# Small loads of one head's V: six rows and 192 keys instead of five rows and 128

## The chip, the cores and the metric

The kernel runs on one core of a Trainium2 chip. The metric is the device time of one execution in microseconds; the number given for a kernel is the median of its runs. A profile is taken of one further execution. "Granted clock" is the share of full speed that TensorE was allowed.

The core's engines are TensorE (PE, with its weight loads as PEld), VectorE (DVE), ScalarE (ACT), GpSimd (POOL) and SyncE (SP). Data come from the chip's memory (HBM) through 16 DMA engines. Here SyncE issues nearly all loads, on one queue.

## The reference

A decode step of two layer kinds, each done twice: attention over the last 1,024 positions of a key and value cache, and a gated feed-forward block. Four sequences, one token each, all in float32.

```python
def _A_ref(x, k_cache, v_cache, wq, wo):          # x 4 x 1 x 640, 32 heads of 128
    W = min(4096, max(256, Sk // 4))              # 1024
    q = (x @ wq).reshape(B, Sq, Hq, Dh)...
    k = k_cache[:, :, Sk - W:, :]
    v = v_cache[:, :, Sk - W:, :]
    scores = einsum("bhqd,bhkd->bhqk", q, k) * (Dh ** -0.5)
    p = softmax(scores, axis=-1)
    o = einsum("bhqk,bhkd->bhqd", p, v)
    return o... @ wo
def _B_ref(x, W_gate, W_up, W_down):              # 640 -> 1728 -> 640
    gate = x @ W_gate; up = x @ W_up
    return ((gate * (gate > 0)) * up) @ W_down
x = x + _A_ref(_layernorm(x), ...)
x = x + _B_ref(_layernorm(x), ...)
x = x + _A_ref(_layernorm(x), ...)
x = x + _B_ref(_layernorm(x), ...)
```

Both layers have the same weights and the same cache. Keys and values of the 1,024 positions are 128 KB x 32 heads x 4 sequences x 2, weights some 25 MB more.

## The kernel before

**Layout.** On the host everything is laid out as long rows of float32 on 128 partitions: `heads` (queries' weights, keys, values and output weights of most heads, in order of use), `kept` (those of the last two groups of heads, which stay on chip between the layers), `mlp`, and `limbs` (below). One head's V is 4,096 columns: eight blocks of 128 keys, each block 512 columns (four sequences of 128), with the key within the block on the partition.

**Store and plan.** `store` is one big tile of 50,304 columns (`STORE`) on all partitions, used as a ring. A list `plan`, written out ahead, has every load in order: layer, row, first and last column, place in the store. `stretch` (line 144) fills the main part: it cuts the `heads` row into loads of at most 16,064 columns (`MOST`, 64,256 B in a partition). `load` (line 226) issues from the front of the plan as long as the places are free; a place is freed by `part_done` after the product that read it (the chip's waits follow from that). So all loads stand on SyncE's queue in the order of the plan, and each waits for the space it goes to.

**Heads and values.** Heads are done in groups of up to four. `values` (line 463) multiplies the softmax weights of a group with V: for each head it copies the weights to a tile `pT`, then does eight products, one a block, into the bank `po`. The results of two rows of blocks add up on four groups of 32 rows of `po`.

**The split head.** Head 17 (`SPLIT`) isn't loaded like the others. Its last block of 128 keys (512 columns) isn't in `heads`: the host puts it into `limbs`, as seven runs of keys (`RUNS`), six of 20 and one of 8. The runs stand on partitions 0 to 19 and 32 to 51, in columns of 512 each. Thirteen small loads a layer (`LIMBS`) bring them to the last 2,048 columns of the store (`PART`): eight loads of five rows with 6 KB a row, and five with two rows or one, 2 KB a row. The rows of one load are four partitions apart, for instance 0, 4, 8, 12 and 16. `stretch` puts one of them ahead of the last big load but two of its stretch (up to the end of head 17), six ahead of the last but one, and six ahead of the last.

Because the keys of a run are on other partitions than their weights, `values` first moves the weights for head 17: a product of `to[:, 7]` with columns of the identity for each run (line 476), into a bank, and a copy to `pT` (line 485). Then come seven whole products and seven products over 20 or 8 partitions (line 490). After these, `free` gives the place back.

Of the kernel before, what the change touches and what calls it, by code (L numbers as in the profile page):

```python
# [13 lines left out]
B, D, H, DH, W, F = 4, 640, 32, 128, 1024, 1728  # L14
P = 128
# [11 lines left out]
KV = 4096  # L27
HEADS = [list(range(h, h + 4)) for h in range(0, 24, 4)] + [[24, 25, 26], [27, 28, 29], [30, 31]]
SIDE = 4
# [32 lines left out]
STORE = 50304  # L62
# [8 lines left out]
FIRST, MOST = 32128, 16064  # L71
LAP = 3 * MOST
SPLIT, PART = 17, 2048
LIMBS = [(half + i, 5, 0, 1536) for i in range(4) for half in (0, 32)] + [(i, 2, 1536, PART) for i in range(3)] + [(3, 1, 1536, PART), (7, 1, 1536, PART)]
RUNS = [(half, 20, 512 * s, 40 * s + 20 * (half > 0)) for s in range(3) for half in (0, 32)] + [(0, 8, 1536, 120)]


def size_of(what, i):
    if what == "v" and i == SPLIT:
        return KV - 512  # L80
    return len(HEADS[i]) * D if what == "q" else D if what == "o" else KV


def fewest(lo, end, n):

    if n == 1:
        return (0, [end]) if end - lo <= MOST else (n + len(CUTS), [])
    most = min(lo + MOST, end)
    ends = [(most, most not in CUTS)] + [(x, False) for x in CUTS if most - 512 < x < most]
    return min((fewest(hi, end, n - 1)[0] + cut, [hi, *fewest(hi, end, n - 1)[1]]) for hi, cut in ends)  # L90
# [23 lines left out]
def decode_kernel(ctx: ExitStack, tc: tile.TileContext, x, source, out):  # L114
    nc = tc.nc
# [10 lines left out]
    store = big.tile([P, STORE], F32, name="store")  # L126
# [7 lines left out]
    plan = []  # L134

    def put(layer, row, to, *cuts):

        for lo, hi in zip(cuts, cuts[1:]):
            assert 0 < hi - lo <= MOST and to % 64 == 0 and lo % 32 == hi % 32 == 0 and to + hi - lo <= STORE, (row, lo, hi, to)
            plan.append((layer, row, lo, hi, to))  # L140
            to += -(-(hi - lo) // 64) * 64
        return to

    def stretch(layer, lo, end, to):

        loads = []
        for hi in fewest(lo, end, -(-(end - lo) // MOST))[1]:
            if to + hi - lo > LAP:
                to = 0
            loads.append((lo, hi, to))  # L150
            to, lo = to + hi - lo, hi
        last = next(i for i, (lo, hi, _) in enumerate(loads) if lo < at_part("v", SPLIT) + KV - 512 <= hi)
        for i, (lo, hi, at) in enumerate(loads):
            if last - 3 < i <= last:
                half = (i - last + 1) * 6 + 1
                plan.extend((layer, "limbs", p, p + 1, STORE - PART) for p in range(max(half, 0), half + 6))
            put(layer, "heads", at, lo, hi)
        return to

    def at_part(what, i):  # L160
        return WHERE[what, i][1]

    def near(c, row="heads"):

        return max(x for x in ROWS[row][2] if x <= c)
# [9 lines left out]
    to = stretch(0, HELD, turn, FIRST)  # L175
# [7 lines left out]
    f, z, a, q, k = FRONT, STORE - D, AHEAD[0], AWAY[0], BACK[0]  # L183
# [4 lines left out]
    lo = 0  # L188
# [6 lines left out]
    lo = HELD  # L195
# [3 lines left out]
    to = AHEAD[1]  # L199
    for n in 832, 1280, 1024, 2048, 3392:  # L200
        to = put(1, "heads", to, lo, lo + n)
        lo += n
    assert to == HOME
    to = HOME + BACK[1] - BACK[0]
    for n in 4096, 6144, 9728:
        hi = near(lo + n)
        to = put(1, "heads", to, lo, hi)
        lo = hi
    hi = near(lo + 4608)
    to = put(1, "heads", to, lo, hi)  # L210
    lo, hi = hi, near(hi + STORE - to)
    put(1, "heads", to, lo, hi)
    last = near(heads_end - 25216)
    to = stretch(1, hi, last, 0)
    for lo, hi in (last, near(last + 12800)), (near(last + 12800), heads_end):
        to = put(1, "heads", to if to + hi - lo <= STORE else 0, lo, hi)
    cuts = [0, 7040, 12160, GU0 + 3 * GU, WD1 + WD, MLP - 4 * D, MLP - 2 * D, MLP - D, MLP - QUARTER, MLP]
    for lo, hi in zip(cuts, cuts[1:]):
        to = put(1, "mlp", to if to + hi - lo <= STORE else 0, lo, hi)
# [6 lines left out]
    def load():  # L226

        if not held:
            nc.sync.dma_start(out=first_q, in_=source["heads"][:, :HELD])
        while plan:  # L230
            layer, row, lo, hi, to = plan[-1]
            if any(live[to:STORE if row == "limbs" else to + hi - lo]):
                break
            plan.pop()
            if row == "limbs":
                live[to:STORE] = [lo == len(LIMBS) - 1] * PART
                p, n, a, b = LIMBS[lo]
                nc.sync.dma_start(out=store[p:p + 4 * n - 3:4, to + a:to + b], in_=source[row][p:p + 4 * n - 3:4, a:b])  # L238
                continue
            live[to:to + hi - lo] = [True] * (hi - lo)  # L240
            held.setdefault((layer, row), []).append((lo, hi - lo, to))
            nc.sync.dma_start(out=store[:, to:to + hi - lo], in_=source[row][:, lo:hi])
# [27 lines left out]
    def product(out, by, layer, row, lo, n, start, stop, rows=slice(0, P), **how):  # L270

        a = 0
        while a < n:
            t, p, m = place(layer, row, lo + a)
            z = min(n, a + m)
            nc.tensor.matmul(out[:, a:z], by, t[rows, p:p + z - a], start=start and not a, stop=stop and z == n, **how)  # L276
            a = z
# [18 lines left out]
    def part(layer, what, h, lo, n):  # L296
        row, first = WHERE[what, h]
        return layer, row, first + lo, n

    def part_done(layer, what, h, lo, n):  # L300
        row, first = WHERE[what, h]
        done(layer, row, first + lo, n)
# [18 lines left out]
    GAP = SIDE * B - B  # L321
# [6 lines left out]
    po = ps_o.tile([P, 512], F32, name="po")  # L328
# [5 lines left out]
    def bank(n):  # L334

        turn_of[0] ^= 1
        return banks[turn_of[0]][:, :n]
# [5 lines left out]
    ident, sel_q = sel_sb[:, :P], sel_sb[:, P:]  # L343
# [6 lines left out]
    for g in range(4):  # L350
        nc.tensor.matmul(y[32 * g:32 * g + B], ident[:B, :B], probs[:B, g * QUARTER:(g + 1) * QUARTER],
                         start=True, stop=True, tile_position=(0, 32 * g))
# [53 lines left out]
    qp, nm, sums, sc, r, oT = {}, {}, {}, {}, {}, {}  # L406
# [56 lines left out]
    def values(layer, g, last=False):  # L463


        n = len(HEADS[g])
        for i, h in enumerate(HEADS[g]):
            t = pT[i % 2]
            to = t[:, GAP:].rearrange("p (c x) -> p c x", c=8)[:, :, :B]
            nc.vector.tensor_copy(to, pp.rearrange("p j (c x) -> p (j c) x", c=4)[:, :, i:P:32])  # L470
            whole = 7 if h == SPLIT else 8
            if h == SPLIT:
                assert 0 < i < n - 1 and (layer, "limbs") not in [p[:2] for p in plan]
                limbs = bank(4 * B).rearrange("p (s x) -> p s x", s=4)
                for p, m, at, key in RUNS:
                    nc.tensor.matmul(limbs[p:p + m, at // 512], ident[:, key:key + m], to[:, 7],
                                     start=True, stop=True, tile_position=(0, p))
            for c in range(whole):
                a = c % 4
                at = GAP + SIDE * B * c - B * i  # L480
                product(po[32 * a:32 * a + SIDE * B], t[:, at:at + SIDE * B], *part(layer, "v", h, c * 512, 512),
                        start=i == 0 and c < 4, stop=i == n - 1 and c >= 4, tile_position=(0, 32 * a))
                part_done(layer, "v", h, c * 512, 512)
            if h == SPLIT:
                nc.vector.tensor_copy(to[:52, :4], limbs[:52])
                for p, m, first, _ in RUNS:
                    r = slice(p, p + m)
                    a = first // 512 % 2 + p // 16
                    at = GAP + SIDE * B * (first // 512) - B * i
                    nc.tensor.matmul(po[32 * a:32 * a + SIDE * B], t[r, at:at + SIDE * B],  # L490
                                     store[r, STORE - PART + first:STORE - PART + first + 512],
                                     start=False, stop=False, tile_position=(p, 32 * a))
                free(STORE - PART, STORE)
        if last:
            waits[0] = layer == 0
            fill(1, pp[:, 0])
            nc.vector.tensor_copy(gates[:, 2 * P:], po[:, 2 * P:])  # L497
            nc.scalar.copy(gates[:, :2 * P], po[:, :2 * P])
            if layer == 0:
                nc.gpsimd.tensor_copy(pT[0][:, GAP:], store[:, AHEAD[0] + INSIDE:AHEAD[0] + INSIDE + P])  # L500
                rest = AHEAD[1] - AHEAD[0] - INSIDE - P
                nc.vector.tensor_copy(pT[1][:, GAP:GAP + rest], store[:, AHEAD[1] - rest:AHEAD[1]])
                free(*AHEAD)
                nc.scalar.copy(po[:, P:], store[:, BACK[0] + 1024:BACK[0] + 1408])
                nc.scalar.copy(pp[:, :, 256:], away[:, :512].rearrange("p (j n) -> p j n", j=2))
                free(*BACK)
        else:
            nc.scalar.copy(gates, po)  # L508
# [167 lines left out]
    last = first_q[96:96 + B, QUARTER:2 * QUARTER]  # L676
# [58 lines left out]
```

## Time and profile before

| | before |
|---|---|
| median of 3 runs | 729.62 us (729.48 to 730.85) |
| profiled execution, its own time | 729.74 us |
| its span, first to last instruction | 727.9 us |
| granted clock, mean | 0.815 |
| TensorE busy | 450.0 us (62%) |
| VectorE, ScalarE busy | 70.5 us, 54.5 us |
| read from HBM | 310.32 MB, 426 GB/s over the span |
| SyncE's queue: packets, share of 16 DMA engines | 13,392, 99.2% |
| instruction packets (queue q8) | 30, 0.49 MB |
| issues of small loads | 26 (16 of 30 KB, 6 of 4 KB, 4 of 2 KB) |

The profiled execution's own time is 1.8 us over its span. Line numbers are those of the kernel's file; line 276 is in the helper that does most products, lines 238 and 242 are the two issues of loads, small and big. A DMA packet is one contiguous row of a load on one DMA engine. In rows by stretches of time, the first numbers are busy times of PE, PEld, DVE, ACT and POOL with counts, then the granted clock, the mean busy share of the 16 DMA engines and what they moved; a packet counts in the stretch in which it starts, so that a share can be over 1 in a short one.

### The profile page before, as it was taken

What the parts mean: (1) busy time and instruction counts of PE and PEld (TensorE: products, weight loads), DVE (VectorE), ACT (ScalarE), POOL (GpSimd) and SP (SyncE); (2) the same over time, 40 slices, a digit from 0 to 9 for tenths busy, and PEclk for the clock granted to TensorE, in tenths of its full rate; (3) what the DMA queues carried; (4) which work ended last, traced back from release to release, by engine and by line L of the source; (5) the groups of instructions that cost most, each with busy time, mean ns of one, the idle gap of its engine ahead of it and who ended that gap; (6) DMA issues with size and microseconds to landing.
All of it is one profiled execution on the core that took longest, in us unless ns stands there. A gap on an engine that the chain in (4) does not pass through costs nothing.

```text
span 727.9 us, 8368 instructions
## 1 busy us (share of the span) xinstructions
PE 450.0 (62%) x3824; PEld 146.9 (20%) x3824; DVE 70.5 (10%) x217; ACT 54.5 (7%) x102; POOL 2.4 (0%) x14
## 2 busy tenths in 40 slices
PE   3546565654645574619868896475756556558576
PEld 1111111111111121103334241021211012102123
DVE  2010001000010000001111211000000010001011
ACT  2000000000000000000412210000000000000100
POOL 0000000000000000000000000000000000000000
PEclk9567888887777787759999999677777878769989
DMA  9999999999999999999999999999999999999997
GB/s 409 444 394 447 440 444 434 412 435 444 443 428 416 421 457 418 444 422 426 418 414 412 426 431 452 429 441 433 434 423 440 438 436 417 441 444 423 425 420 312
DMA packets 13442, 310.91 MB, mean 427 GB/s; under 512 B 1576, under 2 KB 1916, under 8 KB 7136
## 3 DMA queue, kind: packets, MB, share of 16 engines
q1 hardware_dynamic: 13392, 310.37, 99.2%
q8 instruction: 30, 0.49, 0.2%
q14 instruction: 4, 0.03, 0.0%
q10 hardware_dynamic: 16, 0.01, 0.0%
HBM read 310.32 MB, written 0.05 MB: 426 GB/s over the span
## 4 chain that ended last, share of the span: by engine, by line
DMA 77%; PE 20%; DVE 1%; issue 1%; SPq 1%; ACT 0%; DVEq 0%; ACTq 0%
DMA store<-in_heads 62%; DMA store<-in_kept 9%; PE ps L276 8%; DMA store<-in_mlp 6%; PE po L276 6%; PE m L276 2%; PE y L276 1%; PE pp L276 1%; PE pp L461 1%; PE po L490 0%; PE m L432 0%; SPq L238 0%; PE po L358 0%; PE m L521 0%; PE m L512 0%
## 5 line engine op out<-in xcount | busy, mean ns | idle before, releaser
L276 PE MATMUL po<-store,pT 128*16 128x512 f32 x1026 | 157.9, 711 | 120.9 <-DMA store<-in_heads 115.2
L276 PE MATMUL ps<-store,qT 128*4 128x512 f32 (+2 forms) x998 | 152.7, 698 | 101.0 <-DMA store<-in_heads 80.7
L276 PEld LDWEIGHTS po<-store,pT 128*16 128x16 f32 x1026 | 33.4, 109 | 229.5 <-DMA store<-in_heads 126.7
L276 PEld LDWEIGHTS ps<-store,qT 128*4 128x4 f32 x998 | 30.8, 94 | 204.3 <-DMA store<-in_heads 91.8
L457 ACT ACTIVATE probs<-ps,nm 128x1024 f32<-128x1024 f32 x17 | 18.9, 1113 | 334.6 <-DVE nm L453 334.6
L453 DVE TENSOR_REDUCE nm<-ps 128x1 f32<-128x1024 f32 x17 | 20.8, 1225 | 233.9 <-PE ps L276 233.9
L276 PE MATMUL m<-store,xT 128*32 128x512 f32 (+3 forms) x146 | 27.9, 580 | 20.8 <-DMA store<-in_heads 20.8
L276 PE MATMUL y<-store,oT 128*4 128x160 f32 x512 | 23.2, 313 | 10.2 <-DMA store<-in_heads 8.9
L508 ACT COPY gates<-po 128x512 f32<-128x512 f32 x16 | 9.4, 586 | 256.5 <-PE po L276 256.5
L276 PE MATMUL pp<-store,xT 128*32 128x256 f32 (+2 forms) x320 | 20.3, 351 | 9.2 <-DMA store<-in_mlp 4.7
L470 DVE COPY pT<-pp 128x32 f32<-128x32 f32 x64 | 10.3, 184 | 143.5 <-PE po L276 126.4
L461 PE MATMUL pp<-sel_sb,probs 128*128 128x128 f32 x144 | 21.3, 297 | 0.0
L461 PEld LDWEIGHTS pp<-sel_sb,probs 128*128 128x128 f32 x144 | 18.7, 156 | 0.0
L514 DVE RECIPROCAL r<-m 128x16 f32<-128x16 f32 x18 | 4.6, 257 | 123.5 <-PE m L512 123.5
L276 PEld LDWEIGHTS y<-store,oT 128*4 128x4 f32 x512 | 12.7, 89 | 18.4 <-DMA store<-in_heads 9.2
L425 DVE TENSOR_SCALAR gates<-m,rstd 128x512 f32<-128x512 f32 (+2 forms) x18 | 12.4, 690 | 27.1 <-PE m L276 27.1
L276 PEld LDWEIGHTS pp<-store,xT 128*32 128x32 f32 x320 | 10.4, 109 | 17.7 <-DMA store<-in_mlp 8.5
L432 PE MATMUL m<-sel_sb,gates 128*128 128x128 f32 x64 | 12.7, 324 | 0.3 <-DVE gates L425 0.3
L276 PEld LDWEIGHTS m<-store,xT 128*32 128x32 f32 x146 | 6.0, 113 | 32.4 <-DMA store<-in_heads 23.3
L521 PE MATMUL m<-sel_sb,gates 128*128 128x128 f32 x72 | 11.9, 288 | 0.8 <-DVE gates L497 0.8
L432 PEld LDWEIGHTS m<-sel_sb,gates 128*128 128x128 f32 x64 | 7.9, 160 | 19.7 <-issue 18.9
L276 PE MATMUL y<-store,gates 128*4 128x160 f32 (+2 forms) x188 | 9.8, 296 | 1.7 <-DMA store<-in_mlp 1.1
(91 smaller groups left out, 135.7 us busy)
## 6 DMA issues: line engine op xcount, KB each, us to landing
store<-in_heads SPq DMA_DIRECT2D x15, 7936.0 KB
store<-in_heads SPq DMA_DIRECT2D x6, 8032.0 KB
store<-in_heads SPq DMA_DIRECT2D x2, 8000.0 KB
store<-in_heads SPq DMA_DIRECT2D x1, 7872.0 KB
store<-in_heads SPq DMA_DIRECT2D x1, 7424.0 KB
store<-in_heads SPq DMA_DIRECT2D x1, 7360.0 KB
store<-in_heads SPq DMA_DIRECT2D x1, 7168.0 KB
store<-in_heads SPq DMA_DIRECT2D x1, 6400.0 KB
```

Source lines behind the costliest of these rows:

```text
L276: nc.tensor.matmul(out[:, a:z], by, t[rows, p:p + z - a], start=start and not a, stop=stop and z == n, **how)
L425: nc.vector.tensor_scalar(gates[:, :len(HEADS[g]) * P], qp.pop(g), rstd, SCALE, op0=ALU.mult, op1=ALU.mult)
L432: nc.tensor.transpose(qt[:, i], gates[:, i * P:(i + 1) * P], ident)
L453: nc.vector.tensor_reduce(nm[g], to.rearrange("p j n -> p (j n)"), axis=AX.X, op=ALU.max, negate=True)
L457: nc.scalar.activation(probs, sc.pop(g).rearrange("p j n -> p (j n)"), AF.Exp, bias=nm.pop(g), accum_out=sums[g])
L461: nc.tensor.transpose(pp[:, c // 4, c % 4 * P:c % 4 * P + P], probs[:, c * P:(c + 1) * P], ident)
L470: nc.vector.tensor_copy(to, pp.rearrange("p j (c x) -> p (j c) x", c=4)[:, :, i:P:32])
L508: nc.scalar.copy(gates, po)
L514: nc.vector.reciprocal(r[g], so.rearrange("p (b i) -> p i b", b=B)[:, :SIDE])
L521: nc.tensor.transpose(ot[:, 127 * b:127 * b + P], gates[:, b * P:(b + 1) * P], ident)
```

## The change

Head 17's V keeps six whole blocks in `heads`. The seventh block and the eighth are split: 192 of their 256 keys, the whole eighth block and the first 64 keys of the seventh, go through the small loads, now eight runs of 24 keys on partitions 0 to 23 and 32 to 55. There are eight loads of six rows with 8 KB a row. The other 64 keys of the seventh block stay on partitions 64 to 127 and come in one load of 64 rows with 2 KB a row. That makes nine small loads a layer, three ahead of each of the same three big loads.

Since the `heads` row is 512 columns shorter, some big loads of the two stretches are cut elsewhere: in layer 0 the three after the small loads have rows of 62,976, 63,488 and 63,488 B where they had 64,256, 64,256 and 63,488; in layer 1 six loads from the first of these on have 63,488, 64,256, 64,256, 63,488, 63,488 and 51,200 B, before 64,256 four times, 64,000 and 51,200.

In `values`, head 17 takes nine products to move weights (a run can have keys of both blocks), six whole products, one over partitions 64 to 127 and eight over 24 partitions.

```diff
-LIMBS = [(half + i, 5, 0, 1536) for i in range(4) for half in (0, 32)] + [(i, 2, 1536, PART) for i in range(3)] + [(3, 1, 1536, PART), (7, 1, 1536, PART)]
-RUNS = [(half, 20, 512 * s, 40 * s + 20 * (half > 0)) for s in range(3) for half in (0, 32)] + [(0, 8, 1536, 120)]
+LIMBS = [(half + i, 6, 4, 0, PART) for i in range(4) for half in (0, 32)] + [(64, 64, 1, 0, 512)]
+RUNS = [(half, 512 * s) for s in range(4) for half in (0, 32)]
+MOVES = [(*RUNS[i], 24, 7, 24 * i) for i in range(5)] + [(*RUNS[6], 24, 6, 0), (*RUNS[7], 24, 6, 24), (*RUNS[5], 24, 6, 40), (*RUNS[5], 8, 7, 120)]
...
-        return KV - 512
+        return KV - 1024
...
-                half = (i - last + 1) * 6 + 1
-                plan.extend((layer, "limbs", p, p + 1, STORE - PART) for p in range(max(half, 0), half + 6))
+                plan.extend((layer, "limbs", p, p + 1, STORE - PART) for p in range(len(LIMBS)) if p // 3 == i - last + 2)
...
-                p, n, a, b = LIMBS[lo]
-                nc.sync.dma_start(out=store[p:p + 4 * n - 3:4, to + a:to + b], in_=source[row][p:p + 4 * n - 3:4, a:b])
+                p, n, by, a, b = LIMBS[lo]
+                rows = slice(p, p + by * (n - 1) + 1, by)
+                nc.sync.dma_start(out=store[rows, to + a:to + b], in_=source[row][rows, a:b])
...
-            whole = 7 if h == SPLIT else 8
+            whole = 6 if h == SPLIT else 8
...
-                for p, m, at, key in RUNS:
-                    nc.tensor.matmul(limbs[p:p + m, at // 512], ident[:, key:key + m], to[:, 7],
+                for p, at, m, c, key in MOVES:
+                    nc.tensor.matmul(limbs[p:p + m, at // 512], ident[:, key:key + m], to[:, c],
                                      start=True, stop=True, tile_position=(0, p))
...
-                nc.vector.tensor_copy(to[:52, :4], limbs[:52])
-                for p, m, first, _ in RUNS:
-                    r = slice(p, p + m)
+                at = GAP + SIDE * B * 6 - B * i
+                nc.tensor.matmul(po[64:64 + SIDE * B], t[64:, at:at + SIDE * B], store[64:, STORE - PART:STORE - PART + 512],
+                                 start=False, stop=False, tile_position=(64, 64))
+                nc.vector.tensor_copy(to[:56, :4], limbs[:56])
+                for p, first in RUNS:
+                    r = slice(p, p + 24)
```

The host's part lays the same keys out in `limbs`, now 128 rows.

More of the change, by code (lines that the diff above doesn't have):

```diff
@@ L151, in stretch @@
             to, lo = to + hi - lo, hi
-        last = next(i for i, (lo, hi, _) in enumerate(loads) if lo < at_part("v", SPLIT) + KV - 512 <= hi)
+        last = next(i for i, (lo, hi, _) in enumerate(loads) if lo < at_part("v", SPLIT) + KV - 1024 <= hi)
         for i, (lo, hi, at) in enumerate(loads):
             if last - 3 < i <= last:
-                half = (i - last + 1) * 6 + 1
-                plan.extend((layer, "limbs", p, p + 1, STORE - PART) for p in range(max(half, 0), half + 6))
+                plan.extend((layer, "limbs", p, p + 1, STORE - PART) for p in range(len(LIMBS)) if p // 3 == i - last + 2)
             put(layer, "heads", at, lo, hi)
@@ L698 @@
     }
-    split = parts["v"][SPLIT][:, KV - 512:]
-    parts["v"] = [v[:, :KV - 512] if h == SPLIT else v for h, v in enumerate(parts["v"])]
-    limbs = np.zeros((64, PART), np.float32)
-    for p, m, at, key in RUNS:
-        limbs[p:p + m, at:at + 512] = split[key:key + m]
+    split = parts["v"][SPLIT].reshape(P, 8, 512)
+    parts["v"] = [v[:, :KV - 1024] if h == SPLIT else v for h, v in enumerate(parts["v"])]
+    limbs = np.zeros((P, PART), np.float32)
+    for p, at, m, c, key in MOVES:
+        limbs[p:p + m, at:at + 512] = split[key:key + m, c]
+    limbs[64:, :512] = split[64:, 6]
     laid = {row: np.concatenate([parts[what][i] for what, i in row_of], axis=1) for row, row_of in PARTS.items()}
```

## The prediction

> **What bounds the kernel now.** I read the page first: the DMA queues' shares and the chain that ended last.
>
> ```profile
> q1 hardware_dynamic: 13392, 310.37, 99.2%
> q8 instruction: 30, 0.49, 0.2%
> ...
> DMA 77%; PE 20%; DVE 1%; issue 1%; SPq 1%; ACT 0%; DVEq 0%; ACTq 0%
> ```
>
> Then stretches of the span, with the mean busy share of the 16 DMA engines and GB/s as the last two columns, and the end of the chain of waits.
>
> ```profile
> 0.00:345.00 345.00, 190.63 (x1434) 56.86 (x1438) 29.11 (x87) 18.78 (x31) 1.77 (x11) 0.78 1.00 430
> 425.00:720.00 295.00, 189.19 (x1570) 59.49 (x1568) 26.02 (x84) 16.78 (x32) 0.00 (x0) 0.80 1.00 432
> ...
> 693.76 30.76 DMA store<-in_mlp
> 724.52 0.04 issue
> ```
>
> In both attention stages all 16 engines move bytes without a pause. The last load lands at 724.52 us; what follows (some products, the store) runs to 727.9 and isn't touched. So the time is the queue of the DMA engine that finishes last, and the next view asks how far apart they finish. Each row is a short stretch at the end; a share under 1 is engines that have run dry.
>
> ```profile
> 721.00:721.50 0.50, 0.00 (x0) 0.00 (x0) 0.00 (x0) 0.00 (x0) 0.00 (x0) 1.00 1.03 416
> 721.50:722.00 0.50, 0.29 (x11) 0.26 (x14) 0.00 (x0) 0.00 (x0) 0.00 (x0) 1.00 0.87 350
> 722.00:722.50 0.50, 0.50 (x24) 0.42 (x16) 0.00 (x0) 0.00 (x0) 0.00 (x0) 1.00 0.90 352
> 722.50:723.00 0.50, 0.48 (x16) 0.11 (x5) 0.00 (x0) 0.00 (x0) 0.00 (x0) 1.00 0.67 251
> 723.00:723.50 0.50, 0.07 (x4) 0.07 (x8) 0.33 (x1) 0.00 (x0) 0.00 (x0) 1.00 0.47 179
> 723.50:724.00 0.50, 0.50 (x20) 0.34 (x24) 0.00 (x0) 0.00 (x0) 0.00 (x0) 1.00 0.44 158
> 724.00:724.40 0.40, 0.40 (x16) 0.08 (x6) 0.00 (x0) 0.00 (x0) 0.00 (x0) 1.00 0.32 83
> ```
>
> The first engines run dry soon after 721.5 (call it 721.7), the last at 724.4. The missing share, 0.5 x (0.13 + 0.10 + 0.33 + 0.53 + 0.56) + 0.4 x 0.68, is 1.1 us: with the same bytes in the same packets, perfect levelling at the end would be worth 1.1 us and no more. That is 0.15%, and about 0.2% (1.46 us) is the least that a measurement of this kernel tells from no change.
>
> **What sets the engines apart.** The page's 30 instruction packets share the engines with the data. Below are counts of packets in three stretches around 195 us, where the engines pass from one big load to the next, and where the first small load of layer 0 stands. A packet under 512 B is an engine's completion write of a load; one under 8 KB that isn't under 2 KB is a row of a small load.
>
> ```profile
> DMA packets 28, 0.67 MB, mean 1112 GB/s; under 512 B 14, under 2 KB 14, under 8 KB 18
> ...
> DMA packets 2, 0.01 MB, mean 10 GB/s; under 512 B 1, under 2 KB 1, under 8 KB 2
> ...
> DMA packets 12, 0.39 MB, mean 551 GB/s; under 512 B 6, under 2 KB 6, under 8 KB 6
> ```
>
> These are 195.0 to 195.6, 195.6 to 196.2 and 196.2 to 196.9 us. Completions of the small load taken off (4, 0 and 1), ten engines pass early, one between, five late by some 1.35 us, the distance of the stretches' middles (195.3 and 196.6). The five small rows are four in the early stretch, one in the middle: they stand on five different engines (a row takes a quarter of a microsecond, so one engine wouldn't leave such a gap), and none of them is late. Five instruction packets had gone by; here are some of the 30, each alone in a stretch of 10 ns, so that share x 16 x 10 ns is its duration.
>
> ```profile
> 108.72:108.73 0.01, 0.01 (x6) 0.00 (x0) 0.00 (x0) 0.00 (x0) 0.00 (x0) 1.00 5.78 1638
> 249.63:249.64 0.01, 0.00 (x0) 0.00 (x0) 0.00 (x0) 0.00 (x0) 0.00 (x0) 1.00 5.51 1638
> 445.48:445.49 0.01, 0.01 (x2) 0.00 (x0) 0.00 (x0) 0.00 (x0) 0.00 (x0) 1.00 5.78 1638
> 609.51:609.52 0.01, 0.01 (x2) 0.00 (x0) 0.00 (x0) 0.00 (x0) 0.00 (x0) 0.50 5.49 1638
> 684.34:684.35 0.01, 0.01 (x1) 0.00 (x0) 0.00 (x0) 0.00 (x0) 0.00 (x0) 1.00 5.81 1638
> ```
>
> They are the 3rd, 8th, 19th, 24th and 27th: 0.92, 0.88, 0.92, 0.88 and 0.93 us. The duration comes back with a distance of eight or sixteen, so I take it that eight engines fetch instructions in turn. After the eighth, and after layer 0's small loads, the engines pass the next mark like this (251.4 to 252.2, 252.2 to 252.9, 252.9 to 254.8 us):
>
> ```profile
> DMA packets 9, 0.23 MB, mean 286 GB/s; under 512 B 3, under 2 KB 3, under 8 KB 3
> ...
> DMA packets 5, 0.06 MB, mean 91 GB/s; under 512 B 0, under 2 KB 0, under 8 KB 0
> ...
> DMA packets 67, 0.69 MB, mean 364 GB/s; under 512 B 13, under 2 KB 13, under 8 KB 13
> ```
>
> Three engines lead, up to 2.7 us ahead of the last, then nothing, then thirteen. That fits 8 that fetched, 5 that had the small loads, and 3 with neither. In layer 1, at its first small load (583.9 to 584.6, to 585.2, to 585.7, to 586.6 us), it is:
>
> ```profile
> DMA packets 15, 0.28 MB, mean 402 GB/s; under 512 B 7, under 2 KB 7, under 8 KB 11
> ...
> DMA packets 6, 0.19 MB, mean 321 GB/s; under 512 B 3, under 2 KB 3, under 8 KB 3
> ...
> DMA packets 4, 0.07 MB, mean 141 GB/s; under 512 B 2, under 2 KB 2, under 8 KB 3
> ...
> DMA packets 18, 0.58 MB, mean 643 GB/s; under 512 B 9, under 2 KB 9, under 8 KB 9
> ```
>
> Small loads' completions taken off: four engines of the five, then two others, then the fifth, then nine within 0.9 us.
>
> **The change, part by part.** Prices of a row, each alone in 10 ns: 62 KB, a completion write, 6 KB, 2 KB and 8 KB.
>
> ```profile
> 189.67:189.68 0.01, 0.01 (x2) 0.00 (x0) 0.00 (x0) 0.00 (x0) 0.00 (x0) 1.00 14.64 6349
> 195.34:195.35 0.01, 0.00 (x0) 0.00 (x0) 0.00 (x0) 0.00 (x0) 0.00 (x0) 0.50 0.06 0
> 214.29:214.30 0.01, 0.00 (x0) 0.00 (x0) 0.00 (x0) 0.00 (x0) 0.00 (x0) 0.50 1.46 614
> 234.89:234.90 0.01, 0.00 (x0) 0.00 (x0) 0.00 (x0) 0.00 (x0) 0.00 (x0) 0.50 0.53 205
> 405.15:405.16 0.01, 0.01 (x4) 0.00 (x0) 0.00 (x0) 0.01 (x2) 0.00 (x0) 1.00 1.93 819
> ```
>
> That is 2.342, 0.010, 0.234, 0.085 and 0.309 us. In each layer:
>
> Every engine loses its eight 2 KB pieces of the second block that leaves the long rows: 8 x 2.342 x 2,048 / 63,488 = -0.604 us. The load of 64 rows gives back four rows and a completion, 4 x 0.085 + 0.010 = +0.350. The row of before nearest to it is the load of 128 rows with 16 completions; were it on eight engines, those would have 0.69 each and the others nothing, which is the other bound. Small loads: before, five engines had 8 x (0.234 + 0.010) = 1.95, the first and second 0.475 and 0.285 more (five and three 2 KB rows); after, six have 8 x (0.309 + 0.010) = 2.55. Sums: engines seven to sixteen -0.25; third to fifth +0.35; second +0.06; first -0.13; **the sixth +2.30**. Twice that over both layers: -0.51, +0.69, and +4.6 for the sixth. The bytes in all are the same.
>
> [...]
>
> TensorE and the queues, from these rows of the products and of the chain:
>
> ```profile
> L490 PE MATMUL po<-store,pT 20*16 20x512 f32 x24 | 5.5, 819 | 0.0
> L476 PE MATMUL m<-pT,sel_sb 128*20 128x4 f32 x24 | 0.6, 167 | 0.0
> ...
> 605.61 0.70 SPq L238
> ...
> 609.08 35.60 DMA store<-in_heads
> ```
>
> Seven whole and seven partial products become six, one of 64 rows and eight: one more, 0.82 us, and two more moves at 0.17, about 1.2 us a layer; the copy of 56 partitions is that of 52. Cover: the load issued at 609.08 lands 35.6 us later, though its 64,256 B rows need 8 x 2.37 = 19 us, so the queue holds some 16 us of work before it. A 1.2 us later release costs nothing; without cover it would be 2.4 in all. SyncE issues 9 small loads a layer, not 13, three ahead of each big load where there were 1, 6 and 6: its queue gets shorter, under the same cover, price nothing.
>
> **The sum** for the forecast, where the sixth engine is one of the three with neither load nor fetch. In layer 0 it leads by up to 2.7, so +2.30 still isn't last. It keeps nothing of this: its lead at 584 is 1.3, though the others fetched more meanwhile (at least 1.35), so such engines waited some 2.7 us between the layers, and the 2.30 comes out of that wait. In layer 1, as one of the two early ones, it would end at 721.7 + 2.3 = 724.0; as the third, which stood among the nine, at 724.4 to 725.3 (it doesn't take part in the last round of fetches: 724.4 - 1.35 - 0 to 0.9, + 2.3, and 0.25 that the others gain doesn't help it). The fetching engines end at 724.4 - 0.5 = 723.9. The late one of the five: some 1.0 before the last at 585.4, 1.95 of small loads, a fetch of 1.35 less than the last has, so 724.0 now, and +0.35 to +0.69: 724.35 to 724.7. The last of all these is 724.0 to 725.3; I take 724.3, **0.1 us less** than 724.4. The profiled execution took 729.74 us (span 727.9, 1.8 around it), 0.12 over the median of 729.62; 729.74 - 0.1 = **729.6**, own range 729.0 to 730.7.
>
> **Rivals.**
> *The sixth engine fetches instructions.* Then it never waits, ends between 722.5 and 724.4 now, and has the whole +4.6: 727.1 to 729.0, which is 2.7 to 4.6 later, **732.4 to 734.3**. For it: eight of the eleven engines beside the five do fetch. [...] It decides from the point where the sixth's lead in layer 1 is under 2.3 us.
>
> [...]
>
> *SyncE's issues are on the path*, as the chain has them: 605.61 to 609.08 is 3.5 us for six, and three at 0.7 would save 1.4 a layer: **727 to 728.4**. Against: the engines' share is 1.00 all through, with 16 us queued.
>
> **How the numbers follow.** Forecast 0.64, the fetching sixth 0.20, half speed 0.12, issues 0.04. Only the last is faster by over 0.2%, and levelling can't be: faster 0.03. Slower: the fetching sixth and a bit of the others' upper ends, 0.21. No difference 0.76. The range runs from 729.0 into the lower part of the fetching case, 732.8, and leaves out under 0.2.
>
> **What would show it.** At the end, a share that falls from 1 over about 2.5 us again, with the last load at 724 to 725. Wrong if one engine alone runs for 2 us or more past the others (share near 1/16), which is the sixth; for half speed, 2 KB rows of 0.17 instead of 0.085; for SyncE, the engines' share under 1 before a load. In layer 0 at about 252 us two engines should lead, not three.

## The result, and the profile after

The changed kernel takes 735.61 us (median of 6 runs, 734.84 to 735.74) against 729.62 for the kernel before, measured beside it. The ratio is 1.0079, with a 95% interval of 1.0069 to 1.0090: it is **slower by 5.0 to 6.6 us**, 6.0 by the medians. The forecast was 729.6, and the range ended at 732.8. The rival nearest to the result is the fetching sixth engine (732.4 to 734.3), and even that stops 1.3 us short. Three executions among all the runs below (788, 974 and 1,286 us) are slow ones, which are left out of the ranges and ratios; without the last of them the median of 729.48 below would be 729.38.

The page of the changed kernel, its DMA queues (packets, MB, share of 16 engines) and the chain that ended last:

```profile
q1 hardware_dynamic: 13552, 310.37, 98.9%
q8 instruction: 30, 0.49, 0.2%
...
DMA 77%; PE 21%; DVE 1%; issue 0%; ACT 0%; SPq 0%; DVEq 0%; ACTq 0%
```

The bytes are the same and the instruction packets are as many. The 16 engines are still busy almost all through, and DMA still has 77% of the chain. The 160 packets more are the load of 64 rows: 64 rows and 16 completions in each layer. So the added time is longer work on the DMA engines, or work that is spread worse among them. The end shows the second kind. These are stretches of 1 us, the engines' busy share and GB/s last:

```profile
723.00:724.00 1.00, 1.00 (x24) 0.55 (x20) 0.00 (x0) 0.00 (x0) 0.00 (x0) 0.95 1.01 411
724.00:725.00 1.00, 1.00 (x24) 0.22 (x16) 0.10 (x1) 0.37 (x1) 0.00 (x0) 0.95 0.93 385
725.00:726.00 1.00, 1.00 (x32) 0.65 (x28) 0.56 (x2) 0.00 (x0) 0.00 (x0) 0.95 0.93 373
726.00:727.00 1.00, 0.50 (x16) 0.11 (x5) 0.00 (x0) 0.00 (x0) 0.00 (x0) 0.95 0.75 293
727.00:728.00 1.00, 0.44 (x16) 0.40 (x20) 0.00 (x0) 0.00 (x0) 0.00 (x0) 0.95 0.46 172
728.00:729.00 1.00, 0.86 (x26) 0.42 (x16) 0.08 (x1) 0.00 (x0) 0.00 (x0) 0.95 0.12 43
729.00:730.00 1.00, 0.69 (x20) 0.53 (x24) 0.25 (x1) 0.00 (x0) 0.00 (x0) 0.95 0.14 40
```

Before, the share fell from 1 to the end within 2.7 us (721.7 to 724.4). Here it begins to fall at about 724, is at 0.12 from 728 on, and the last load lands at 730.3. One engine is 0.06. The counts of packets from 728.0 to 728.9 and from 728.9 to 730.3 us tell how many engines are left (under 512 B is an engine's completion write of a load):

```profile
DMA packets 33, 0.04 MB, mean 45 GB/s; under 512 B 6, under 2 KB 27, under 8 KB 33
...
DMA packets 24, 0.05 MB, mean 34 GB/s; under 512 B 3, under 2 KB 19, under 8 KB 23
```

The last three completions, at 729.36, 729.97 and 730.20 us, come one after another: they are the last three loads on **one engine**, which ends 1.55 us after the next one (728.65). In the kernel before, the last two completions were 0.09 us apart (724.26 and 724.35). But the others are late too: the next to last engine ends 4.3 us later than the last one did before. Whether one loaded engine can be behind both, this view doesn't tell; the first run below does. (No record names the engine of a packet. But a packet starts within some 6 ns of another's end: in the kernel before, a row of 64,256 B starts at 202.219 us where one ends at 202.223. So where the engines stand apart, one can be followed from packet to packet.)

### The profile page after: what moved, and what is told of

Its sections match the earlier page's. It is cut to its first block, busy times and chain, and to the rows that moved or that the text cites. A ratio compares the mean times of both kernels' runs of the same rounds, so it can differ in the third digit from the quotient of the medians.

```text
span 733.7 us, 8367 instructions
## 1 busy us (share of the span) xinstructions
PE 458.9 (63%) x3830; PEld 145.0 (20%) x3830; DVE 70.4 (10%) x217; ACT 54.5 (7%) x102; POOL 2.4 (0%) x14
## 4 chain that ended last, share of the span: by engine, by line
DMA 77%; PE 21%; DVE 1%; issue 0%; ACT 0%; SPq 0%; DVEq 0%; ACTq 0%
DMA store<-in_heads 62%; DMA store<-in_kept 8%; PE ps L277 8%; DMA store<-in_mlp 6%; PE po L277 6%; PE y L277 2%; PE m L277 2%; PE pp L277 1%; PE pp L462 1%; PE m L433 1%; PE po L494 0%; PE m L525 0%; PE po L359 0%; PE po L487 0%; PE po L366 0%
## 5 line engine op out<-in xcount | busy, mean ns | idle before, releaser
L277 PE MATMUL po<-store,pT 128*16 128x512 f32 x1018 | 161.1, 725 | 121.7 <-DMA store<-in_heads 115.6
L277 PE MATMUL ps<-store,qT 128*4 128x512 f32 (+2 forms) x996 | 156.1, 710 | 98.2 <-DMA store<-in_heads 77.5
```

## The experiments

Three theories stood. **A**: the sixth engine, the one that has the sixth row of a small load, fetches instructions, so the added small-load rows on it (4.6 us in both layers) have nothing to hide behind. **B**: the load of 64 rows, all in the upper half of the partitions, makes other packets longer. **C**: something else in the change costs time, since the sum doesn't close with A and B. The rows and the load of 64 rows can be undone one by one, which gives a table of four.

**Six rows alone, on the kernel before.** The eight loads of five rows become six rows of the same 6 KB; they hold the same 128 keys (`RUNS` is cut to match), and the five odd small loads go. No block leaves the long rows, and no load of 64 rows is there.

```diff
-LIMBS = [(half + i, 5, 0, 1536) for i in range(4) for half in (0, 32)] + [(i, 2, 1536, PART) for i in range(3)] + [(3, 1, 1536, PART), (7, 1, 1536, PART)]
+LIMBS = [(half + i, 6, 0, 1536) for i in range(4) for half in (0, 32)]
...
```

> The kernel before with one part of the change: eight small loads of six rows, 6 KB a row, bring the same 128 keys; block seven stays in the big loads, and there is no load of 64 rows. The five-row loads' 1.95 us a layer on five engines become 1.95 on six. Theory A (the sixth engine is one of those that fetch instructions, and the last to finish): +3.9 less a lead of 0.2 to 0.5, so 733.1 to 733.5 us. Theory B (the load of 64 rows alone makes the loss): 729.6, no change. Theory C (rows of 8 KB or the new cut of the big loads make it): 729.6 too.

Measured: 733.13 us (731.80 to 733.66), ratio 1.0048 (1.0035 to 1.0061). The sixth engine gets 2 x 8 x 0.244 = 3.9 us more by the rows' price, and the kernel is 3.5 us slower, within what was expected of A. The counts below are of this kernel in the same three stretches around the first small load of layer 0 that the prediction read (195.0 to 195.6, 195.6 to 196.2, 196.2 to 196.9 us):

```profile
DMA packets 26, 0.60 MB, mean 1005 GB/s; under 512 B 13, under 2 KB 13, under 8 KB 17
...
DMA packets 4, 0.07 MB, mean 117 GB/s; under 512 B 2, under 2 KB 2, under 8 KB 3
...
DMA packets 12, 0.33 MB, mean 468 GB/s; under 512 B 6, under 2 KB 6, under 8 KB 7
```

"Under 8 KB" less "under 2 KB" are the small rows: 4, 1 and 1. Before, they were 4, 1 and 0. The sixth row stands in the late stretch, among the five engines that are late by about 1.35 us because they have fetched instructions: five packets had gone by, of 0.93 to 0.97 us each in the kernel before. **The sixth engine is one of the eight that fetch.** Followed from packet to packet, the engine whose first small row starts at 196.70 us leads back to an instruction packet at 108.71, the third of the 30; the five others carry none between 104 and 252 us. In the changed kernel's own trace the sixth row, at 196.64 us, leads back to the third one too, at 108.65. The prediction had named another sign: at about 252 us two engines should lead instead of three, if the sixth had been one of the idle three. From 251.4 to 252.2, to 252.9 and to 254.8 us this kernel has:

```profile
DMA packets 9, 0.18 MB, mean 223 GB/s; under 512 B 3, under 2 KB 3, under 8 KB 3
...
DMA packets 5, 0.11 MB, mean 164 GB/s; under 512 B 0, under 2 KB 0, under 8 KB 0
...
DMA packets 61, 0.63 MB, mean 330 GB/s; under 512 B 12, under 2 KB 12, under 8 KB 12
```

Three still lead: the sixth row was not put on any of them.

This run also answers the question left open above. Two pieces of the chain of waits in the feed-forward block between the layers, first in the kernel before, then here, and two stretches of the end here:

```profile
377.38 7.58 DMA store<-in_mlp
...
379.42 7.61 DMA store<-in_mlp
...
726.00:727.00 1.00, 0.79 (x24) 0.37 (x16) 0.15 (x1) 0.00 (x0) 0.00 (x0) 1.00 0.25 90
727.00:728.00 1.00, 0.76 (x24) 0.49 (x24) 0.18 (x1) 0.00 (x0) 0.00 (x0) 1.00 0.06 24
```

The chain waits there for whole loads, and the same load lands 2.1 us later. In layer 1 everything is later by that much or a little more: the first small row, which is another engine's, starts at 586.48 us, before at 584.03. So what the sixth engine got in layer 0 had been handed on to all engines between the layers. What it got in layer 1 stays with it: the next to last engine ends at 726.83 us, and from there to 728.18 a single one is busy (share 0.06). Followed back, this one carries eight small rows of layer 1 and an instruction packet at 688.40 us: the sixth. One loaded engine can thus make the others late as well, by 2.5 us here (726.83 against 724.35).

**The changed kernel with five rows.** Four slots of 8 KB in five rows hold 160 keys; 32 of head 17's keys, the last four of each run, are left out of the computation. The load of 64 rows stays.

```diff
-LIMBS = [(half + i, 6, 4, 0, PART) for i in range(4) for half in (0, 32)] + [(64, 64, 1, 0, 512)]
+LIMBS = [(half + i, 5, 4, 0, PART) for i in range(4) for half in (0, 32)] + [(64, 64, 1, 0, 512)]
...
```

> The changed kernel with five rows in the small loads instead of six; it leaves out 32 of head 17's keys, and the load of 64 rows stays. Theory A alone: the sixth engine has nothing extra, so 729.3 to 729.7. Theory B: the loss of the packets that the 64-row load makes longer stays (some 0.9 us a layer on each engine as the changed kernel's trace has it, less the 0.25 that each gains), so 730.7 to 731.3; if it were the whole loss, 735.

Measured: 731.81 us (731.24 to 732.70), ratio 1.0032 (1.0021 to 1.0044). Most of the loss goes with the sixth row, but more is left than B had been given.

**The changed kernel without the load of 64 rows** and its product; its 64 keys are left out.

```diff
-LIMBS = [(half + i, 6, 4, 0, PART) for i in range(4) for half in (0, 32)] + [(64, 64, 1, 0, 512)]
+LIMBS = [(half + i, 6, 4, 0, PART) for i in range(4) for half in (0, 32)]
...
-                nc.tensor.matmul(po[64:64 + SIDE * B], t[64:, at:at + SIDE * B], store[64:, STORE - PART:STORE - PART + 512],
-                                 start=False, stop=False, tile_position=(64, 64))
```

> The changed kernel without the load of 64 rows and its product; it leaves out 64 of head 17's keys. Theory A: the sixth engine has 2.55 - 0.60 = 1.95 more a layer than before, 3.9 less a lead of 0.2 to 0.5: 733.1 to 733.5. Theory B alone: 729.3 to 729.7. Both in part: between, and the difference to the changed kernel is the load of 64 rows (0.35 of its own and what it does to others, a layer).

Measured: 733.48 us (733.17 to 734.23), ratio 1.0056 (1.0042 to 1.0069). The median lies in A's range; the 2.1 us that the load of 64 rows then costs are three times its own 0.7.

**Both undone**: five rows and no load of 64 rows; 96 keys are left out.

```diff
-LIMBS = [(half + i, 6, 4, 0, PART) for i in range(4) for half in (0, 32)] + [(64, 64, 1, 0, 512)]
+LIMBS = [(half + i, 5, 4, 0, PART) for i in range(4) for half in (0, 32)]
...
```

> The changed kernel with five rows and without the load of 64 rows; it leaves out 96 of head 17's keys. Eleven engines have 0.60 us less a layer than before, five have 2.55 - 0.60 = 1.95, as before. If theories A and B are all of the loss: 728.4 to 729.4. If the rows of 8 KB, the new cut of the big loads or the other order of issue cost anything (theory C): 730 or more.

Measured: 729.48 us (729.11 to 730.33), ratio 0.9996 (0.9987 to 1.0005). That is at the upper end of the range given for A and B, and below C's 730. C falls: with both undone nothing of the loss is left. Eleven engines have 1.2 us less to do here over both layers, and the time doesn't show it, because the five of the small loads keep theirs (-0.604 + 2.55 - 1.95 = 0 a layer). The end of this kernel:

```profile
721.00:722.00 1.00, 0.40 (x12) 0.36 (x16) 0.00 (x0) 0.00 (x0) 0.00 (x0) 1.00 0.84 337
722.00:723.00 1.00, 0.87 (x28) 0.45 (x16) 0.06 (x1) 0.00 (x0) 0.00 (x0) 1.00 0.69 265
723.00:724.00 1.00, 0.68 (x20) 0.43 (x24) 0.27 (x1) 0.00 (x0) 0.00 (x0) 1.00 0.33 118
724.00:725.00 1.00, 0.85 (x20) 0.20 (x8) 0.00 (x0) 0.03 (x1) 0.00 (x0) 1.00 0.08 22
```

The share falls earlier than in the kernel before, but the last engine still ends soon after 724.

The four together, medians in us:

```
                 no load of 64 rows   with it     the load's part
five rows              729.48          731.81        +2.33
six rows               733.48          735.61        +2.13
the sixth row's part    +4.00           +3.80
```

The two parts add up: 4.00 + 2.33 = 6.33, where both together cost 6.13. Within 0.2 us, nothing of the 6 us is left for a third cause. The sixth row is worth about 4 us, within what the rival priced (2.7 to 4.6). The load of 64 rows is worth 2.1 to 2.3, where the forecast gave it 0.7, its own work.

**What the load of 64 rows does.** In the trace of the changed kernel, single packets around it, each in its own 10 ns (share x 16 x 10 ns is the duration):

```profile
234.13:234.14 0.01, 0.00 (x0) 0.00 (x0) 0.00 (x0) 0.00 (x0) 0.00 (x0) 0.50 0.53 205
234.26:234.27 0.01, 0.00 (x0) 0.00 (x0) 0.00 (x0) 0.00 (x0) 0.00 (x0) 0.50 20.27 6350
234.63:234.64 0.01, 0.00 (x0) 0.00 (x0) 0.00 (x0) 0.00 (x0) 0.00 (x0) 0.50 1.07 205
235.67:235.68 0.01, 0.00 (x0) 0.00 (x0) 0.00 (x0) 0.00 (x0) 0.00 (x0) 0.50 3.18 819
627.56:627.57 0.01, 0.00 (x0) 0.00 (x0) 0.00 (x0) 0.00 (x0) 0.00 (x0) 0.50 21.45 6349
```

A row of 2 KB can take 0.171 us instead of 0.085, the sign that the prediction had named for half speed. But this is an exception: of the 64 rows, 50 in layer 0 and 37 in layer 1 take 0.09 us or less, like the first one shown, and three and four take 0.15 or more. A small load's row of 8 KB takes 0.509 instead of 0.309, and the neighbouring loads' rows of 62 KB take about 3.2 and 3.4 (completions stand in these stretches too) instead of 2.342. Added up over the packets of 228 to 242 us that are longer than their kind's usual duration, that is 14.4 us of engine time, and some 15 us in 621 to 634. The 2 KB rows have 0.6 and 1.0 us of this, the long rows of the big loads 12.5 and 13.1. Around the other small loads of layer 0, with no 64 rows near, it is 1.0 us (190 to 204 us), as in the kernel before, and nothing (208 to 222).

Two runs were to put a price on this by themselves, on the kernel before: one load more a layer of 64 rows of 2 KB that nothing reads, on partitions 64 to 127 and then on 32 to 95.

```diff
-LIMBS = [(half + i, 5, 0, 1536) for i in range(4) for half in (0, 32)] + [(i, 2, 1536, PART) for i in range(3)] + [(3, 1, 1536, PART), (7, 1, 1536, PART)]
+LIMBS = [(half + i, 5, 4, 0, 1536) for i in range(4) for half in (0, 32)] + [(i, 2, 4, 1536, PART) for i in range(3)] + [(3, 1, 4, 1536, PART), (7, 1, 4, 1536, PART)] + [(64, 64, 1, 1536, PART)]
...
```

The first is shown; the second has 32 in place of 64 as its first partition. The third number is the distance of the rows.

> The kernel before and one more small load a layer, after the thirteen: 64 rows of 2 KB on partitions 64 to 127, zeros that nothing reads. Its own work is 4 x 0.085 + 0.010 = 0.35 us a layer on each engine. [...]

> [...] Theory B: no packet gets longer, 0.7 us in all, 730.3. If it is 64 rows as such, or the 2 KB rows, that make the loss: as in the other run, 731.5 to 732.5.

Measured: 738.38 us (737.93 to 738.90) and 737.36 us (737.12 to 737.80); both are 4.9 us or more above all that had been expected, for another reason. From 230 to 240 us, the kernel before and then the first:

```profile
230.00:240.00 10.00, 4.00 (x21) 1.32 (x25) 0.00 (x0) 0.00 (x0) 0.00 (x0) 0.54 0.97 419
...
230.00:240.00 10.00, 3.59 (x25) 1.38 (x29) 0.00 (x0) 0.00 (x0) 0.00 (x0) 0.66 0.68 254
```

and the second:

```profile
230.00:240.00 10.00, 3.75 (x21) 1.33 (x25) 0.00 (x0) 0.00 (x0) 0.00 (x0) 0.55 0.65 248
```

The engines run dry: a share of 0.68 and 0.65, where the kernel before has 0.97. The big load behind the small ones is issued at 236.4 us and at 236.3, where the kernel before issues it at 219.6: with a fourteenth small load SyncE waits before it can issue the next, 16.2 us in the first of the two, which the trace puts down to the landing of an earlier big load. (Why it waits for that one wasn't tried.) So these two give no price for the 64 rows. A third run was to find which engines fetch, with ten small loads more a layer of 6 to 15 rows; it met the same wait:

> The kernel before and ten more small loads a layer, of 6, 7 and so on up to 15 rows, 2 KB a row, zeros that nothing reads. [...]

Measured: 768.38 us, one run, against 729.53 beside it. Its engines run dry for longer:

```profile
230.00:240.00 10.00, 3.87 (x21) 1.32 (x25) 0.00 (x0) 0.00 (x0) 0.00 (x0) 0.50 0.37 157
240.00:250.00 10.00, 6.28 (x86) 2.44 (x78) 1.54 (x4) 1.20 (x2) 0.00 (x0) 0.98 0.06 13
```

With engines standing still, the rows can't be told apart by engine. Beyond the sixth, which engines fetch stays open.

**A clean trio.** To keep nine small loads or fewer, the base has eight loads of five rows with 6 KB (120 keys) and leaves out 136 of the head's keys; its fourth slot is free for a load of 64 rows that nothing reads. The products are the same in all three.

```diff
-LIMBS = [(half + i, 5, 4, 0, PART) for i in range(4) for half in (0, 32)]
-RUNS = [(half, 512 * s) for s in range(4) for half in (0, 32)]
-MOVES = [(*RUNS[i], 24, 7, 24 * i) for i in range(5)] + [(*RUNS[6], 24, 6, 0), (*RUNS[7], 24, 6, 24), (*RUNS[5], 24, 6, 40), (*RUNS[5], 8, 7, 120)]
+LIMBS = [(half + i, 5, 4, 0, 1536) for i in range(4) for half in (0, 32)]
+RUNS = [(half, 512 * s) for s in range(3) for half in (0, 32)]
+MOVES = [(*RUNS[i], 20, 7, 20 * i) for i in range(6)]
...
```

That is the base against the run with both parts undone; the two others have `(32, 64, 1, 1536, PART)` or `(64, 64, 1, 1536, PART)` as a ninth load.

> The base of a pair. In each layer eight small loads of five rows of 6 KB (three slots of 2 KB, 120 keys) and no load of 64 rows; it leaves out 136 of that head's keys a layer. Against the kernel before, every engine loses 0.604 us a layer and the five engines of the small loads at least as much. If the five set the end in the run without the half load (they had 2.55 - 0.604 against 1.95 there, the same as before), both kinds now lose 1.2 us over two layers: 728.2 to 728.9. If the time is held by something that is not the engines' queues, 729.3 to 729.7.

> The base with one load of 64 rows of 2 KB a layer, on partitions 32 to 95, half in each half of the partitions; nothing reads it. Its own work is 0.35 us an engine and layer. [...] By the rival, that any load of 64 short rows beside long rows costs 1.17 us a layer: the base + 2.3.

> The same load on partitions 64 to 127, the place that the change gives it; nothing reads it. [...] By the rival: the same as on 32 to 95, within 0.3.

Measured, medians of 10 to 11 runs: the base 728.75 us (ratio 0.9986, 0.9977 to 0.9995), on 32 to 95 **729.40** (0.9998, 0.9989 to 1.0007), on 64 to 127 **731.00** (1.0022, 1.0012 to 1.0031). The load costs 0.65 us in the one place, about its own work (2 x 0.35 = 0.70), and 2.25 us in the other. The rival's times, 2.3 over the base in both places, are missed by 1.6 us on 32 to 95. The rows, bytes and number of loads are the same; only the partitions differ. In the four microseconds in which nearly all of the 64 rows stand in layer 0 (232.4 to 236.4 us) the changed kernel has

```profile
232.40:236.40 4.00, 0.00 (x0) 0.00 (x0) 0.00 (x0) 0.00 (x0) 0.00 (x0) 0.50 1.05 366
```

The load on 64 to 127, with a 62 KB row and a 2 KB row beside it:

```profile
232.40:236.40 4.00, 0.30 (x4) 0.11 (x8) 0.00 (x0) 0.00 (x0) 0.00 (x0) 0.50 1.08 381
...
232.53:232.54 0.01, 0.00 (x0) 0.00 (x0) 0.00 (x0) 0.00 (x0) 0.00 (x0) 0.50 18.62 6349
...
234.40:234.41 0.01, 0.00 (x0) 0.00 (x0) 0.00 (x0) 0.00 (x0) 0.00 (x0) 0.50 0.99 205
```

The load on 32 to 95, the same:

```profile
232.40:236.40 4.00, 1.22 (x8) 0.26 (x12) 0.00 (x0) 0.00 (x0) 0.00 (x0) 0.50 0.87 365
...
232.70:232.71 0.01, 0.00 (x0) 0.00 (x0) 0.00 (x0) 0.00 (x0) 0.00 (x0) 0.50 14.64 6349
234.13:234.14 0.01, 0.00 (x0) 0.00 (x0) 0.00 (x0) 0.00 (x0) 0.00 (x0) 0.50 0.53 205
```

The base:

```profile
232.40:236.40 4.00, 0.91 (x8) 0.21 (x12) 0.00 (x0) 0.00 (x0) 0.00 (x0) 0.50 0.92 396
```

Divide the GB/s by the share, and it is what the engines move while they are busy: 349 in the changed kernel, 353 on 64 to 127, 420 on 32 to 95, 430 without the load. With the load on the upper half the engines carry 18% less while they are busy (1 - 353 / 430); over four microseconds that is 0.7 us a layer. The runs gave (2.25 - 0.65) / 2 = 0.8. The 62 KB row shown takes 2.98 us on 64 to 127 and 2.342 on 32 to 95, the 2 KB row 0.158 and 0.085. Of the 64 rows in this layer seven take 0.15 or more on 64 to 127, and one on 32 to 95. Counted as above, the added engine time is 12.6 and 9.0 us in the two layers on 64 to 127, less than the changed kernel's 14.4 and 15, and 1.2 and 0 on 32 to 95.

So the place alone makes the difference: 2.25 us against 0.65. What in the place makes it, these runs don't show.

## Why the prediction was wrong

**What bounds the kernel**: right. The queue of the engine that ends last sets the time. The end moved from 724.4 to 730.3, and the span by 5.8 us with it.

**The prices of the edits**: right, except for one. Between the base and the run with both parts undone, five engines differ by 2 x 8 x (0.309 - 0.234) = 1.2 us, and the time by 0.73 (a ratio to before of 0.9996 against 0.9986). That fits if the five end last in the one run and others in the other; which engines these are wasn't followed in the trace. The sums go by the engines' places, the first to the sixteenth, and give the first and second 0.475 and 0.285 us for rows of 2 KB; no run shows in what order a load takes the engines. What the runs showed in its place: five rows stand on five engines and the sixth row on one more, which has eight such rows in layer 1 of the run with six rows alone, and a load of 64 rows has 16 completions (160 packets more over both layers). The sum for the third to fifth (zero without the load of 64 rows) was met within 0.2 us (729.48 against 729.65 beside it). The own work of the load of 64 rows was put at 2 x 0.350 = 0.70, and is 0.65 where its rows stand in both halves. (The product more was priced at 0.82 us, the mean duration of one of the two instructions that make up such a product. They overlap: 24 of them are busy for 5.5 us, 0.46 a product. Nothing hangs on it, as no time of TensorE showed.)

**The step that failed** is "the sixth engine is one of the three with neither load nor fetch". The rival's reasoning held: its range of 2.7 to 4.6 us later contains the 3.5 to 4.0 measured. What was wrong is the role given to this engine, and the chance of 0.20 for the other role. I had counted, from the trace, eight fetching engines among the eleven beside the five. That alone gives any one of the eleven 8/11 = 0.73. I set it aside for a guess about the order of the engines, for which no row spoke. By the count, the rival would have been the forecast. The trace of before couldn't decide it: its small loads have five rows at most, so there was no sixth row to follow. The first trace with a load of six rows decides it. The sign named for it, one engine alone for 2 us or more, came only in part: it is 1.55 us in the changed kernel and 1.35 with six rows alone, because the burden of layer 0 had reached all engines by then.

**The second step that failed** is the price of the 64 rows in the upper half. The forecast gave them their own work alone, 0.35 us a layer. The 0.12 for half speed stood for 2 KB rows of 0.17 us instead of 0.085, which would be another 4 x 0.085 = 0.34 a layer on an engine; that was my estimate, and the trace shows 0.15 us or more for three and four of the 64 rows. It was right that the upper half costs more (2.25 us against 0.65 in the clean trio); where the cost falls was wrong. Most 2 KB rows kept their 0.085 us; what got longer is the long rows that other loads have under way. In the changed kernel 14 to 15 us of engine time are added a layer, where the 64 rows at half speed would add 64 x 0.085 = 5.4. The excess is 0.8 us a layer in the clean trio instead of 0.34. How a row of one load holds up a row of another, no run shows. I took a dearer load of 64 rows and the fetching sixth engine as alternatives besides. They held together: even at 0.34 a layer the two reach to 734.3 + 0.7 = 735.0, and the range stopped at 732.8.

**The cover of TensorE's products and of SyncE's issues**: nothing in the runs speaks against it within a stage. Between the layers the products do wait for whole loads, so an engine that is late there makes all the others late, by some 2.5 us in the run with six rows alone; the sum had no such term, as its sixth engine was early. The table of four leaves at most 0.2 us for all else. That SyncE's issues aren't on the path is right with nine loads; with fourteen they are, which the prediction had no reason to see.

**Levelling**: no gain was to be had and none came. The kernel with both parts undone reads 96 keys less a layer and is still no faster than the one before.

## What to carry to other kernels

Where engines differ in what they carry, a small load with one more row is one more engine loaded, and if that one is already among the last, its price shows almost whole: 3.9 us more on that engine over two layers cost 3.5 to 4.0 us of 730 here. When the trace tells how many engines have some burden but not which, take the chance from the count. And a load of 64 rows beside long ones was better placed across the two halves of the partitions (0.65 us over two layers); inside the upper half (2.25 us) it slowed down what the other loads had under way: a row of 62 KB shown took 2.98 us there and 2.342 across the halves (the lower half wasn't tried).

## What the runs showed of the hardware

- A load of 64 short rows in partitions 64 to 127 lengthens packets of other loads: in the changed kernel rows of 62 KB go from 2.342 us up to 3.4, 14 to 15 us of engine time a layer, while 87 of its own 128 rows of 2 KB take 0.09 us or less. Read by nothing, such a load costs 2.25 us over both layers on partitions 64 to 127 and 0.65 on 32 to 95.
- Engines are not alike: as counted from the trace of before, eight of the 16 also fetch instructions, in packets of 16 KB. The packets' durations come back with a distance of eight (the 3rd, 11th, 19th and 27th of 30 take 0.925, 0.924, 0.925 and 0.929 us, the 7th, 15th and 23rd 0.879, 0.879 and 0.881), and at 252 us, after eight of them and the small loads on five engines, three engines lead. In the run with six rows alone the engine with the sixth row carries the third packet. Of the 30, 28 take 0.88 to 0.97 us and two 1.08 and 1.16. A fetch costs its engine more than that: behind the one at 202.40 us (0.948 us) the next row of 64,256 B takes 2.851 us instead of 2.371, so the engine is late by some 1.4 us.
- With a fourteenth small load in a layer, an issue of SyncE went from 219.6 to 236.4 us and the DMA engines ran dry (share 0.68 over 10 us).
